# The first tile's x in another order: first weight chunk converted early, two k shifts on GpSimd, and the next k two slots later

## The chip, the cores and the metric

The kernel runs on one core of one Trainium2 chip. The metric is the device time of one execution in microseconds (us); shorter is better. TensorE is called PE here, VectorE DVE, ScalarE ACT, GpSimd POOL and SyncE SP, as in the profile. All four compute engines and SP's DMA queue run their own instruction lists in order and meet at semaphores.

## The reference

A linear attention over q, k and v of 8 batches, 8 heads, 576 positions and 64 columns feeds a two-layer feed-forward over 4608 tokens:

```python
q_s = softmax of q over its 64 columns          # exp(q - max) / (sum + 1e-9)
k_s = softmax of k over its 576 positions
kv  = einsum('bhsd,bhse->bhde', k_s, v)
x   = einsum('bhsd,bhde->bhse', q_s, kv)        # as [4608, 512]
h   = x @ w_in                                  # [4608, 2048]
out = softplus(h) @ w_out                       # [4608, 512]
```

Everything is float32 outside. Weights arrive as float32 bits in 64-bit words and are converted on the chip.

## The kernel before, in words

The 4608 tokens are cut into nine tiles of 512. For each tile the feed-forward runs sixteen **slots**, one for each 128 columns of the hidden layer (a **chunk**). A slot j issues, in this order: the up-projection of chunk j on PE (`up`, L367 in the first tile, L372 to L374 later), the attention steps of the next tile that a table puts into this slot, the conversion steps of the coming weight chunks, softplus of chunk j (`softplus`, L384 to L390 on ACT and DVE), and the down-projection of chunk j - 2 (`down`, L412). Products on PE that an attention step needs are gathered (`later`) and issued at the end of the slot. The work of one slot on each engine stands in that engine's list in the order of this code; no scheduler moves it.

**The weights.** In the first tile each chunk must be converted before it is used. `top_w` (L120) and `scale_w` (L115) on ACT, `sign_w` on DVE (L126) or, for chunks 0 and 1, on POOL (L128), and last `join_w` on DVE (L136). `top_w` reads both halves of a chunk, so it waits for the load of w_in and of w_out. Chunks 0 and 1 are converted ahead of the slots, chunk j + 2 after softplus of slot j, and `join_w(j + 1)` stands between the attention steps and softplus of slot j. Up-projection j + 1 waits for it.

**The attention.** `kv_unit` makes kv for one batch and two heads (index h, four per batch). Its steps are numbered u*h*0 to u*h*5: `top` (maximum over chunks of k, L182, and a transpose on PE, L184), `across` (maximum over the partitions, L198, and a transpose back, L199), `shift` (k minus its maximum, L203), `product` (exp on ACT, L209, twenty matmuls, L214), `scale` (L224, L225) and `keep` (L232) or `split` (L238, L241). `q_unit` has twelve steps q0 to q11: maxima (L278), an exchange between partition blocks (`swapped`, four small copies into the tile `other`, L265) with L287, the shift (L290), exp (L293), sums (L296), the second exchange and the reciprocal (L300, L301), and the division (L304). `x_first` makes x of the first tile, steps x*h*0 to x*h*2: `flip` (transpose, L348), `product` (L351), `take` (copy to x0, L355 on ACT, L357 on DVE).

**The head of the program**, up to the first up-projection, is a string of step names written out by hand; each name appends its instructions to the lists of the engines. t, m, s and j with a digit are `top_w`, `scale_w`, `sign_w` on POOL and `join_w` of chunk 0 or 1, "kv", "w" and "q" issue loads. k of the first batch lies in the tiles kvt, kvt, x_130 and x_136 for h = 0 to 3. In `attend(1)` the four kv units of the second batch are spread over the slots of the first tile from slot 2h on, two slots apart; each one's product also starts a later k load into the buffer that it frees.

Of the kernel before, what the change touches and what calls it, by code (L numbers as in the profile page):

```python
# [8 lines left out]
F32 = mybir.dt.float32  # L9
# [10 lines left out]
P = 128  # L20
B, H, S, D = 8, 8, 576, 64
DM, DF = 512, 2048
NT = B * S
HP = H // 2
# [30 lines left out]
def tile_attn_ffn(  # L55
# [9 lines left out]
    nc = tc.nc  # L65
# [8 lines left out]
    sm = ctx.enter_context(tc.tile_pool(name="sm", bufs=1))  # L74
# [76 lines left out]
    def later(products):  # L151
        if waiting is None:
            products()
        else:
            waiting.append(products)
# [14 lines left out]
        queue.dma_start(out=t[0:TAIL, NCH, :, 0:2 * D], in_=kv_tail[b, h])  # L170
        return t

    def kv_unit(b, h, bank, after=None):

        t = loaded.pop((b, h))
        kt, vt = t[:, :, :, 0:D], t[:, :, :, D:KVW]
        wide, ps = bank[:, 0:P], bank[:, 0:D + 1]
        state = {}

        def top():  # L180
            mx = sm.tile([P, 2, D], F32, name="mx", bufs=2)
            nc.vector.tensor_reduce(out=mx, in_=kt.rearrange("p c z d -> p z d c"), op=ALU.max, axis=AX.X)  # L182
            if b <= ON_PE:
                later(lambda: nc.tensor.transpose(wide, mx.rearrange("p z d -> p (z d)"), ident))  # L184
                return
            mb = sm.tile([P, 2, D], F32, name="mx", bufs=2)
            nc.gpsimd.partition_all_reduce(
                mb.rearrange("p z d -> p (z d)"), mx.rearrange("p z d -> p (z d)"), channels=P,
                reduce_op=bass_isa.ReduceOp.max,
            )  # L190
            state["mb"] = mb

        def across():

            if b > ON_PE:
                return
            m1 = sm.tile([P, 1], F32, name="m1", bufs=2)
            nc.vector.tensor_reduce(out=m1, in_=wide, op=ALU.max, axis=AX.X)  # L198
            later(lambda: nc.tensor.transpose(wide, m1.broadcast_to([P, P]), ident))  # L199

        def shift():
            mb = wide.rearrange("p (z d) -> p z d", z=2) if b <= ON_PE else state["mb"]
            nc.vector.tensor_tensor(  # L203
                out=kt, in0=kt, in1=mb.unsqueeze(1).broadcast_to([P, NCH + 1, 2, D]), op=ALU.subtract
            )

        def product():
            cz = t.rearrange("p c z w -> p (c z) w")[:, :, 0:D]
            nc.scalar.activation(cz, cz, AF.Exp)  # L209

            def products():
                for c in range(NCH + 1):
                    for z in range(2):
                        nc.tensor.matmul(  # L214
                            ps[z * D:(z + 1) * D], lhsT=kt[:, c, z], rhs=vt[:, c, z], start=c == 0, stop=c == NCH
                        )
                if after:
                    after()

            later(products)  # L220

        def scale():
            r = sm.tile([P, 1], F32, name="r", bufs=2)
            nc.vector.tensor_scalar(out=r, in0=ps[:, D:D + 1], scalar1=EPS, scalar2=W_SCALE, op0=ALU.add, op1=ALU.mult)  # L224
            nc.vector.reciprocal(r, r)  # L225
            state["r"] = r

        def keep():

            for z in range(2):  # L230
                zs = slice(z * D, (z + 1) * D)
                nc.scalar.activation(whole[zs, h, zs], ps[zs, 0:D], AF.Copy, scale=state["r"][zs])  # L232

        def split():
            hi, lo, r = kv_hi[b % 2][h], kv_lo[b % 2][h], state["r"]
            for z in range(2):
                zs = slice(z * D, (z + 1) * D)
                nc.scalar.activation(hi[zs, zs], ps[zs, 0:D], AF.Copy, scale=r[zs])  # L238
            for z in range(2):
                zs = slice(z * D, (z + 1) * D)  # L240
                nc.vector.scalar_tensor_tensor(  # L241
                    out=lo[zs, zs], in0=ps[zs, 0:D], scalar=r[zs], in1=hi[zs, zs].bitcast(F32),
                    op0=ALU.mult, op1=ALU.subtract,
                )

        return [top, across, shift, product, scale, split if b else keep]

    def split_whole(h):
# [11 lines left out]
    def swapped(m, copy=nc.vector.tensor_copy):  # L260

        o = sm.tile([P, TOK // 8], F32, name="other")
        for a in range(4):
            z = a ^ 1
            copy(o[32 * a:32 * a + 32], m[32 * z:32 * z + 32])  # L265
        return o

    def q_unit(t):

        n = TOK // 16  # L270
        half = [qtiles[t][:, 2 * g:2 * g + 2].rearrange("p h (i r) -> p (h i) r", r=32) for g in range(2)]
        m, s = (sm.tile([P, TOK // 8], F32, name=name) for name in ("m", "s"))

        def spread(a, g):
            return a[:, g * n:(g + 1) * n].unsqueeze(2).broadcast_to([P, n, 32])

        def top(g):
            nc.vector.tensor_reduce(out=m[:, g * n:(g + 1) * n], in_=half[g], op=ALU.max, axis=AX.X)  # L278

        copy = nc.vector.tensor_copy if t else nc.scalar.copy  # L280
        if t:
            slow = [nc.gpsimd if t == 1 else nc.vector] * 2
        else:
            slow = [nc.vector, nc.gpsimd]

        def join():
            nc.vector.tensor_tensor(out=m, in0=m, in1=swapped(m, copy), op=ALU.max)  # L287

        def shift(g):
            slow[g].tensor_tensor(out=half[g], in0=half[g], in1=spread(m, g), op=ALU.subtract)  # L290

        def power(g):
            nc.scalar.activation(half[g], half[g], AF.Exp)  # L293

        def total(g):
            nc.vector.tensor_reduce(out=s[:, g * n:(g + 1) * n], in_=half[g], op=ALU.add, axis=AX.X)  # L296

        def invert():
            o = swapped(s, copy)
            nc.vector.scalar_tensor_tensor(out=s, in0=s, scalar=EPS, in1=o, op0=ALU.add, op1=ALU.add)  # L300
            nc.vector.reciprocal(s, s)  # L301

        def divide(g):
            slow[g].tensor_tensor(out=half[g], in0=half[g], in1=spread(s, g), op=ALU.mult)  # L304

        return [
            lambda: top(0), lambda: top(1), join, lambda: shift(0), lambda: shift(1),
            lambda: power(0), lambda: power(1), lambda: total(0), lambda: total(1), invert, lambda: divide(0), lambda: divide(1),
        ]
# [131 lines left out]
    with tc.manual_schedule():  # L441
# [17 lines left out]


        po = [ps_o.tile([P, DM], F32, name=f"po{h}") for h in range(HP)]
        units = [kv_unit(0, h, po[h]) for h in range(HP)]
        first = [x_first(h, po[h]) for h in range(HP)]
        todo = {f"q{i}": fn for i, fn in enumerate(q_unit(0))}
        for h in range(HP):
            todo.update({f"u{h}{i}": fn for i, fn in enumerate(units[h])})
# [5 lines left out]
        todo["w"] = lambda: [load_w(k) for k in range(5, 10)]  # L472
        todo["q"] = lambda: [q_load(1)] + [load_w(k) for k in range(10, NJ)]
        for name in (
            "q0 q1 u00 q2 q3 q4 q5 u10 u01 u11 u02 u12 q6 u03 u13 u20 u30 u21 u31 u22 u32 u23 u33 t0 m0 s0 q7 q8 "
            "kv kv w u04 u14 u05 u15 q9 q10 q11 x00 x10 x01 x11 u24 u34 u25 u35 x20 x30 x02 x12 t1 m1 s1 x21 x31 j0 "
            "x22 x32 q"
        ).split():
            todo[name]()

        def attend(t):

            steps = [[] for _ in range(NJ + 1)]

            def lazy(make, slots):
                unit = []

                def step(i):
                    def fn():
                        if not i:  # L490
                            unit.extend(make())
                        unit[i]()
                    return fn

                for i, s in enumerate(slots):
                    steps[s].append(step(i))

            if t < B:
                on_pe = 1 if t <= ON_PE else 0
                for h in range(HP):  # L500
                    a = 2 * h
                    lazy(
                        lambda h=h: kv_unit(t, h, banks[h % 2], after=kv_prefetch),
                        [a, a + on_pe, a + 1 + on_pe, a + 2 + on_pe, a + 3 + on_pe, a + 3 + on_pe],
                    )
            lazy(lambda: q_unit(t), [3, 4, 5, 5, 6, 7, 8, 7, 8, 9, 9, 10])
            for h, slots in enumerate(([11, 11, 12], [12, 12, 13], [13, 13, NJ], [14, 14, NJ])):
                lazy(lambda h=h: x_unit(t, h, banks[h % 2]), slots)
            if t + 1 < NTILE:
                steps[14].append(lambda: q_load(t + 1))  # L510
            return steps
# [3 lines left out]
        for n in range(len(order) + 3):  # L515
            slot = order[n] if n < len(order) else None
            if slot:
                t, j = slot
# [66 lines left out]
```

## Time and profile before

| | |
|---|---|
| time, median of 3 runs | 929.53 us (928.31 to 929.96) |
| the profiled execution's own time | 928.47 us |
| its span | 926.6 us |
| PE busy | 886.7 us, 96% of the span |
| DVE / ACT / POOL busy | 703.8 (76%) / 581.7 (63%) / 56.4 (6%) us |
| first up-projection starts | 34.55 us |
| first up-projection of the second tile starts | about 160.6 us |

The span is the time from the first to the last instruction; the execution's own time is 1.87 us longer. PE is busy nearly throughout from the second tile on, so the time is PE's work plus what PE waits for in the head and in the first tile. PEclk on the page is the clock granted to TensorE in tenths; it stood at half (0.50, which is 1.2 instead of 2.4 GHz) from about 26 to 32 us and again from about 46 to 49 us.

### The profile page before, as it was taken

Reading aid. Unit: us, or ns where it says so; the run is one execution under the profiler, and the core shown is the slowest. Engines: PE = TensorE matmul, PEld = TensorE weight load, DVE = VectorE, ACT = ScalarE, POOL = GpSimd, SP = SyncE. Lnnn points to the kernel's source line nnn. Section 1 sums busy time; section 2 is a strip of 40 time slices with the busy share of each in tenths; the row PEclk is TensorE's granted clock in tenths of the full one; section 3 lists DMA queues with packets and bytes.
Section 4 is the critical chain, followed back from the end, with each engine's and each line's share of the span. In section 5 each row is a group of like instructions: output and inputs, shape, how many; then the busy total and the mean of one; then the engine's idle time right before and its main releaser. Section 6 shows DMA issues by size and latency. Waiting matters only on the chain.

```text
span 926.6 us, 11575 instructions
## 1 busy us (share of the span) xinstructions
PE 886.7 (96%) x4180; PEld 675.3 (73%) x4180; DVE 703.8 (76%) x1095; ACT 581.7 (63%) x982; POOL 56.4 (6%) x118
## 2 busy tenths in 40 slices
PE   2698999999899999999999999999999999999998
PEld 2243444677688888888888888888888888888886
DVE  8679888788878877787778778877787757765553
ACT  3666676756666656666567566656665666566554
POOL 1302200000001100110011000100110000000000
PEclk9899999999999999999999999999999999999999
DMA  9970101111013101210121012101200110001001
GB/s 315 381 298 26 35 17 46 45 53 52 1 46 97 52 1 46 89 43 18 46 71 52 27 46 71 52 26 46 71 27 1 46 46 1 1 1 46 0 1 46
DMA packets 49034, 55.28 MB, mean 60 GB/s; under 512 B 2256, under 2 KB 39120, under 8 KB 47824
## 3 DMA queue, kind: packets, MB, share of 16 engines
q1 hardware_dynamic: 48400, 54.27, 17.4%
q8 instruction: 33, 0.54, 0.2%
q10 hardware_dynamic: 576, 0.26, 0.1%
q14 instruction: 25, 0.20, 0.1%
HBM read 45.09 MB, written 9.44 MB: 59 GB/s over the span
## 4 chain that ended last, share of the span: by engine, by line
PE 76%; DVE 12%; ACT 8%; issue 3%; DMA 1%; POOL 0%; SPq 0%; DVEq 0%; ACTq 0%; POOLq 0%
PE ph L372 11%; PE ph L374 11%; PE ph L373 11%; PE po L418 11%; PE po L416 11%; PE po L417 11%; PE ph L367 3%; PE po L412 3%; PE att L214 2%; DVE w L126 1%; DVE l L390 1%; DVE w L389 1%; DVE w L388 1%; PE att L331 1%; ACT u L385 1%
## 5 line engine op out<-in xcount | busy, mean ns | idle before, releaser
L372 PE MATMUL ph<-x,w 128*128 128x512 f32 x480 | 191.7, 399 | 0.0
L418 PE MATMUL po<-w,g_lo 128*128 128x512 f32 x480 | 187.0, 390 | 1.4 <-DVE g_lo L396 1.4
L374 PE MATMUL ph<-x,w 128*128 128x512 f32 x480 | 188.0, 392 | 0.0
L373 PE MATMUL ph<-x,w 128*128 128x512 f32 x480 | 187.6, 391 | 0.0
L416 PE MATMUL po<-w,g_hi 128*128 128x512 f32 x480 | 186.8, 389 | 0.0
L417 PE MATMUL po<-w,g_hi 128*128 128x512 f32 x480 | 186.7, 389 | 0.0
L388 DVE SCALAR_TENSOR_TENSOR w<-w,u 128x512 f32<-128x512 f32 x128 | 88.4, 691 | 108.8 <-ACT w L386 108.8
L395 ACT CAST g_hi<-l 128x512 fp32r<-128x512 f32 x128 | 79.7, 622 | 92.3 <-DVE l L390 89.8
L390 DVE SCALAR_TENSOR_TENSOR l<-l,ln,w 128x512 f32<-128x512 f32 x128 | 96.3, 752 | 15.7 <-DVE w L389 1.4
L418 PEld LDWEIGHTS po<-w,g_lo 128*128 128x128 f32 x480 | 90.1, 188 | 21.2 <-DVE g_lo L396 2.6
L372 PEld LDWEIGHTS ph<-x,w 128*128 128x128 f32 x480 | 90.8, 189 | 19.3 <-issue 0.6
L374 PEld LDWEIGHTS ph<-x,w 128*128 128x128 f32 x480 | 90.4, 188 | 19.7
L417 PEld LDWEIGHTS po<-w,g_hi 128*128 128x128 f32 x480 | 90.1, 188 | 18.7
L416 PEld LDWEIGHTS po<-w,g_hi 128*128 128x128 f32 x480 | 90.1, 188 | 18.6
L373 PEld LDWEIGHTS ph<-x,w 128*128 128x128 f32 x480 | 90.7, 189 | 17.6 <-DVE w L146 0.2
L384 ACT ACTIVATE u<-ph 128x512 f32<-128x512 f32 x134 | 80.1, 598 | 33.5 <-PE ph L374 25.0
L396 DVE TENSOR_TENSOR g_lo<-l,g_hi 128x512 fp32r<-128x512 f32 x128 | 88.4, 691 | 15.5 <-ACT g_hi L395 15.3
L387 ACT ACTIVATE l<-u 128x512 f32<-128x512 f32 x128 | 79.3, 619 | 25.8 <-DVE g_lo L396 25.2
L389 DVE SCALAR_TENSOR_TENSOR w<-ph,w 128x512 f32<-128x512 f32 x128 | 88.5, 691 | 4.4
L385 ACT ACTIVATE u<-u 128x512 f32<-128x512 f32 x134 | 84.7, 632 | 4.3
L386 ACT ACTIVATE w<-u 128x512 f32<-128x512 f32 x128 | 80.9, 632 | 4.1
L325 ACT CAST q_hi<-att 128x512 fp32r<-128x512 f32 x32 | 18.8, 587 | 78.6 <-DVE att L321 78.6
(125 smaller groups left out, 1061.1 us busy)
## 6 DMA issues: line engine op xcount, KB each, us to landing
kvt<-in_kv SPq DMA_DIRECT2D x30, 512.0 KB, 4.2
qt<-in_q SPq DMA_DIRECT2D x9, 1024.0 KB, 4.9
w<-in_w_in SPq DMA_DIRECT2D x16, 512.0 KB, 10.2
w<-in_w_out SPq DMA_DIRECT2D x16, 512.0 KB, 10.2
out<-w SPq DMA_DIRECT2D x32, 256.0 KB, 2.3
kvt<-in_kv_tail SPq DMA_DIRECT2D x28, 64.0 KB, 3.9
x<-in_kv SPq DMA_DIRECT2D x2, 512.0 KB, 9.4
out<-x SPq DMA_DIRECT2D x4, 256.0 KB, 2.4
```

The source lines that it names most:

```text
L372: nc.tensor.matmul(ph, lhsT=w_hi, rhs=x_hi, start=h == 0, stop=False)
L373: nc.tensor.matmul(ph, lhsT=w_lo, rhs=x_hi, start=False, stop=False)
L374: nc.tensor.matmul(ph, lhsT=w_hi, rhs=x_lo, start=False, stop=h == HP - 1)
L385: nc.scalar.activation(u, u, AF.Exp, scale=-1.0)
L386: nc.scalar.activation(w, u, AF.Copy, bias=1.0)
L388: nc.vector.scalar_tensor_tensor(out=w, in0=w, scalar=1.0, in1=u, op0=ALU.subtract, op1=ALU.subtract)
L389: nc.vector.scalar_tensor_tensor(out=w, in0=ph, scalar=0.0, in1=w, op0=ALU.max, op1=ALU.subtract)
L390: nc.vector.scalar_tensor_tensor(out=l, in0=l, scalar=ln1, in1=w, op0=ALU.subtract, op1=ALU.add)
L396: nc.vector.tensor_tensor(out=g_lo, in0=l, in1=g_hi.bitcast(F32), op=ALU.subtract)
L416: nc.tensor.matmul(po, lhsT=g_hi[:, ms], rhs=w_hi, start=j == 0, stop=False)
L417: nc.tensor.matmul(po, lhsT=g_hi[:, ms], rhs=w_lo, start=False, stop=False)
L418: nc.tensor.matmul(po, lhsT=g_lo[:, ms], rhs=w_hi, start=False, stop=j == NJ - 1)
```

## The change

Four edits. (1) The string of steps in the head is written in another order: t0 and m0 (the conversion of chunk 0 on ACT) stand right behind the exp of the first half of q, s0 (POOL) before the exp of the second half; the sums' exchange (q9) stands between the work of h = 0 and h = 1; j0 before the last flips; t1, m1, s1 behind the last flips. (2) The shifts of h = 2 and 3 are done by POOL instead of DVE; ACT first copies their maxima from PSUM into the tile mx, which POOL reads. (3) For the second tile's q the exchange copies are on ACT. (4) In the first tile the kv units of the second batch start two slots later.

```diff
--- before.py
+++ after.py
@@ -170,7 +170,7 @@
         queue.dma_start(out=t[0:TAIL, NCH, :, 0:2 * D], in_=kv_tail[b, h])
         return t
 
-    def kv_unit(b, h, bank, after=None):
+    def kv_unit(b, h, bank, engine=nc.vector, after=None):
 
         t = loaded.pop((b, h))
         kt, vt = t[:, :, :, 0:D], t[:, :, :, D:KVW]
@@ -200,7 +200,10 @@
 
         def shift():
             mb = wide.rearrange("p (z d) -> p z d", z=2) if b <= ON_PE else state["mb"]
-            nc.vector.tensor_tensor(
+            if engine is nc.gpsimd:
+                mb = sm.tile([P, 2, D], F32, name="mx", bufs=2)
+                nc.scalar.copy(mb.rearrange("p z d -> p (z d)"), wide)
+            engine.tensor_tensor(
                 out=kt, in0=kt, in1=mb.unsqueeze(1).broadcast_to([P, NCH + 1, 2, D]), op=ALU.subtract
             )
 
@@ -277,7 +280,7 @@
         def top(g):
             nc.vector.tensor_reduce(out=m[:, g * n:(g + 1) * n], in_=half[g], op=ALU.max, axis=AX.X)
 
-        copy = nc.vector.tensor_copy if t else nc.scalar.copy
+        copy = nc.vector.tensor_copy if t > 1 else nc.scalar.copy
         if t:
             slow = [nc.gpsimd if t == 1 else nc.vector] * 2
         else:
@@ -459,7 +462,7 @@
 
 
         po = [ps_o.tile([P, DM], F32, name=f"po{h}") for h in range(HP)]
-        units = [kv_unit(0, h, po[h]) for h in range(HP)]
+        units = [kv_unit(0, h, po[h], engine=nc.vector if h < 2 else nc.gpsimd) for h in range(HP)]
         first = [x_first(h, po[h]) for h in range(HP)]
         todo = {f"q{i}": fn for i, fn in enumerate(q_unit(0))}
         for h in range(HP):
@@ -472,9 +475,8 @@
         todo["w"] = lambda: [load_w(k) for k in range(5, 10)]
         todo["q"] = lambda: [q_load(1)] + [load_w(k) for k in range(10, NJ)]
         for name in (
-            "q0 q1 u00 q2 q3 q4 q5 u10 u01 u11 u02 u12 q6 u03 u13 u20 u30 u21 u31 u22 u32 u23 u33 t0 m0 s0 q7 q8 "
-            "kv kv w u04 u14 u05 u15 q9 q10 q11 x00 x10 x01 x11 u24 u34 u25 u35 x20 x30 x02 x12 t1 m1 s1 x21 x31 j0 "
-            "x22 x32 q"
+            "q0 q1 u00 q2 q3 q4 q5 t0 m0 u10 u01 u11 u02 u12 s0 q6 u03 u13 u20 u30 u21 u31 u22 u32 q7 q8 kv kv w u23 "
+            "u04 u05 q9 u33 u14 u15 q10 q11 x00 x10 x01 x11 j0 x02 u24 u25 u34 u35 x20 x30 x21 x31 x12 t1 m1 s1 x22 x32 q"
         ).split():
             todo[name]()
 
@@ -498,7 +500,7 @@
             if t < B:
                 on_pe = 1 if t <= ON_PE else 0
                 for h in range(HP):
-                    a = 2 * h
+                    a = 2 * h + (2 if t == 1 else 0)
                     lazy(
                         lambda h=h: kv_unit(t, h, banks[h % 2], after=kv_prefetch),
                         [a, a + on_pe, a + 1 + on_pe, a + 2 + on_pe, a + 3 + on_pe, a + 3 + on_pe],
```

On ACT, in the head, before: from the first copies of q's exchange (other<-m) to the second exchange (other<-s). The tile w_142 is chunk 0, spare holds kv, po_179 to po_182 are the PSUM banks of h = 0 to 3.

```order
L265 COPY other<-m 32x64 x4
L293 ACTIVATE qt<-qt 128x1024 x2
L209 ACTIVATE kvt<-kvt 128x10x64 x2
L209 ACTIVATE x_130<-x_130 128x10x64
L209 ACTIVATE x_136<-x_136 128x10x64
L120 ACTIVATE w_142<-w_142 128x1024
L115 ACTIVATE w_142<-w_142 128x1024
L232 ACTIVATE spare<-po_179,r 64x64 x2
L232 ACTIVATE spare<-po_180,r 64x64 x2
L265 COPY other<-s 32x64 x4
```

The same stretch of ACT's list with the change:

```order
L268 COPY other<-m 32x64 x4
L296 ACTIVATE qt<-qt 128x1024
L120 ACTIVATE w_142<-w_142 128x1024
L115 ACTIVATE w_142<-w_142 128x1024
L296 ACTIVATE qt<-qt 128x1024
L212 ACTIVATE kvt<-kvt 128x10x64 x2
L205 COPY mx<-po_181 128x128
L205 COPY mx<-po_182 128x128
L212 ACTIVATE x_130<-x_130 128x10x64
L235 ACTIVATE spare<-po_179,r 64x64 x2
L268 COPY other<-s 32x64 x4
L212 ACTIVATE x_136<-x_136 128x10x64
```

The two instructions on w_142 moved from behind the exps of all four k tiles to a place ahead of the second exp of qt and of all four; two copies into mx are new; the keeping of po_180 went behind the second exchange.

On DVE, in the head, before: from the sums of q to the first flips (w_160 holds the flipped q).

```order
L296 TENSOR_REDUCE s<-qt 128x32 x2
L224 TENSOR_SCALAR r<-po_179 128x1
L225 RECIPROCAL r<-r 128x1
L224 TENSOR_SCALAR r<-po_180 128x1
L225 RECIPROCAL r<-r 128x1
L300 SCALAR_TENSOR_TENSOR s<-s,other 128x64
L301 RECIPROCAL s<-s 128x64
L304 TENSOR_TENSOR qt<-qt,s 128x1024
L348 STREAM_TRANSPOSE w_160<-qt 128x512 x2
```

The same with the change:

```order
L299 TENSOR_REDUCE s<-qt 128x32 x2
L227 TENSOR_SCALAR r<-po_179 128x1
L228 RECIPROCAL r<-r 128x1
L303 SCALAR_TENSOR_TENSOR s<-s,other 128x64
L304 RECIPROCAL s<-s 128x64
L227 TENSOR_SCALAR r<-po_180 128x1
L228 RECIPROCAL r<-r 128x1
L307 TENSOR_TENSOR qt<-qt,s 128x1024
L351 STREAM_TRANSPOSE w_160<-qt 128x512 x2
L136 SCALAR_TENSOR_TENSOR w_142<-w_142 128x1024
```

The two shifts of x_130 and x_136 that stood ahead of these rows are gone from DVE; the sums' reciprocal now stands before the scaling of po_180, and the join of chunk 0 stands behind the first two flips.

On DVE, in slot 8 of the first tile, before: from the end of softplus to the join of the next chunk. att_105 and att_106 are the two PSUM banks of the kv units.

```order
L390 SCALAR_TENSOR_TENSOR g_hi<-g_hi,ln_109,g_lo 128x512
L126 TENSOR_SCALAR w_298<-w_298 128x1024
L224 TENSOR_SCALAR r<-att_105 128x1
L225 RECIPROCAL r<-r 128x1
L241 SCALAR_TENSOR_TENSOR kv_lo_103<-att_105,r,kv_hi_95 64x64 x2
L203 TENSOR_TENSOR kvt<-kvt,att_106 128x10x64
L296 TENSOR_REDUCE s<-qt 128x32
L136 SCALAR_TENSOR_TENSOR w_298<-w_298 128x1024
```

The same with the change:

```order
L393 SCALAR_TENSOR_TENSOR g_hi<-g_hi,ln_109,g_lo 128x512
L126 TENSOR_SCALAR w_280<-w_280 128x1024
L227 TENSOR_SCALAR r<-att_106 128x1
L228 RECIPROCAL r<-r 128x1
L244 SCALAR_TENSOR_TENSOR kv_lo_102<-att_106,r,kv_hi_94 64x64 x2
L206 TENSOR_TENSOR kvt<-kvt,att_105 128x10x64
L182 TENSOR_REDUCE mx<-kvt 128x128
L299 TENSOR_REDUCE s<-qt 128x32
L136 SCALAR_TENSOR_TENSOR w_280<-w_280 128x1024
```

The units' numbers moved on by one (what was h = 2 is h = 1), and a maximum over k, of h = 3, stands between the shift and the sums; before, that one stood two slots earlier.

## Rows read from the trace of the kernel before

**Rows 1.** The windows view, in stages; columns: stretch, length, each engine's busy time, clock, DMA

```profile
0.00:34.55 34.55, 12.42 (x96) 7.21 (x97) 26.64 (x66) 15.96 (x30) 9.21 (x16) 0.90 1.03 327
34.55:160.63 126.08, 117.96 (x352) 52.45 (x353) 105.80 (x141) 84.34 (x122) 13.20 (x17) 0.99 0.31 116
160.63:926.60 765.97, 756.34 (x3734) 615.67 (x3732) 571.33 (x890) 481.43 (x830) 33.94 (x86) 1.00 0.12 38
```

**Rows 2.** One load by its tile: the issue of w_out's first block, and its landing

```profile
L97 SPq DMA_DIRECT2D w<-in_w_out x1: 432/432/432, 10.9 to 10.9; - x1
...
DMA to landing us min/median/max: 6.3/6.3/6.3
```

**Rows 3.** The timeline of ACT, 13 to 26 us; columns: start, duration, instruction, [wait before it]

```profile
13.60 1.06 ACT L293 ACTIVATE qt<-qt 128x1024 f32<-128x1024 f32 x1 [1.12 <-POOL qt L290]
14.56 1.36 ACT L209 ACTIVATE kvt<-kvt 128x640 f32<-128x640 f32 x2
19.94 1.48 ACT L209 ACTIVATE x<-x 128x640 f32<-128x640 f32 x2 [4.02 <-DVE x L203]
21.33 1.14 ACT L120 ACTIVATE w<-w 128x1024 uint32<-128x1024 uint8 x1
22.36 1.12 ACT L115 ACTIVATE w<-w 128x1024 f32<-128x1024 f32 x1
...
24.68 1.00 ACT L265 COPY other<-s 32x64 f32<-32x64 f32 x4
```

**Rows 4.** The timeline of PE, 15 to 39 us

```profile
15.34 2.44 PE L214 MATMUL po<-kvt 128*64 128x65 f32 x40 [1.37 <-ACT kvt L209]
...
18.57 0.59 PE L199 MATMUL po<-ident,m 128*128 128x128 f32 x2 [0.17 <-DVE m L198]
20.74 1.54 PE L214 MATMUL po<-x 128*64 128x65 f32 x40 [1.58 <-ACT x L209]
28.68 5.60 PE L351 MATMUL po<-w,spare 128*128 128x512 f32 x8 [6.40 <-DVE w L348]
34.55 3.68 PE L367 MATMUL ph<-x,w 128*128 128x512 f32 x8 [0.27 <-DVE w L136]
```

**Rows 5.** The timeline of DVE, 20 to 30 us

```profile
20.55 2.34 DVE L296 TENSOR_REDUCE s<-qt 128x32 f32<-128x1024 f32 x2
...
26.57 1.23 DVE L304 TENSOR_TENSOR qt<-qt,s 128x1024 f32<-128x1024 f32 x1
27.82 1.30 DVE L348 STREAM_TRANSPOSE w<-qt 128x512 f32<-128x512 f32 x2
```

**Rows 6.** The timeline of POOL, three of its operations

```profile
11.66 1.90 POOL L290 TENSOR_TENSOR qt<-qt,m 128x1024 f32<-128x1024 f32 x1
...
23.58 2.46 POOL L128 TENSOR_SCALAR w<-w 128x1024 bf16<-128x1024 f32 x1 [10.02 <-ACT w L115]
...
80.64 1.92 POOL L290 TENSOR_TENSOR qt<-qt,m 128x1024 f32<-128x1024 f32 x1
```

**Rows 7.** The timeline of DVE in the first tile's slots

```profile
77.63 2.24 DVE L388 SCALAR_TENSOR_TENSOR g_lo<-g_lo,l 128x512 f32<-128x512 f32 x1
...
80.71 2.40 DVE L390 SCALAR_TENSOR_TENSOR g_hi<-g_hi,ln,g_lo 128x512 f32<-128x512 f32 x1
...
86.66 1.29 DVE L182 TENSOR_REDUCE mx<-kvt 128x128 f32<-128x640 f32 x1
...
100.33 0.20 DVE L224 TENSOR_SCALAR r<-att 128x1 f32<-128x1 f32 x1
...
102.12 0.82 DVE L203 TENSOR_TENSOR kvt<-kvt,att 128x640 f32<-128x640 f32 x1
```

**Rows 8.** The timeline of PE in the first tile: three up-projections that waited

```profile
45.55 5.41 PE L367 MATMUL ph<-x,w 128*128 128x512 f32 x8 [1.01 <-DVE w L136]
...
71.93 3.71 PE L367 MATMUL ph<-x,w 128*128 128x512 f32 x8 [2.09 <-DVE w L136]
...
105.26 3.71 PE L367 MATMUL ph<-x,w 128*128 128x512 f32 x8 [0.79 <-DVE w L136]
```

## The prediction, made before the changed kernel was run

> **What bounds the kernel now.** I read the page's busy shares first, then the windows by stage, and then each engine's timeline of the first 160 us. From 160.63 us on PE is busy 756.34 of 765.97 us, and the change leaves the instructions of that stage and their order as they are [rows 1]. What it can move lies before: 34.55 us of head, in which PE works 12.42, and 126.08 us of the first tile, in which it works 117.96 [rows 1]. In the head the reader is to see a string of hand-overs: exps of k on ACT, products and transposes on PE, maxima and shifts on DVE, the conversion of chunk 0, the second exchange on ACT, the division and the flips on DVE, and then four products at 28.68 that run slowly, 5.60 us for eight instructions of 512 columns where the same shape takes 3.68 right after [rows 3 to 5]. The 6.40 us of idle PE ahead of them, and the page's clock, say that this is the lower level, 1.2 GHz. In the first tile, up-projections wait for the join of their chunk on DVE, the third, sixth and tenth for instance [rows 8]; how long depends on the attention steps that stand ahead of that join.
>
> **The head, step by step.** The part that decides is the conversion of chunk 0 on ACT. Before, it stands at 21.33 and takes 2.04 us to the next instruction's start, on the chain [rows 3]. Now it stands ahead of the second exp of q and the exps of h = 0 and 1. It reads the whole chunk, and its second half was issued at 10.9 and landed 6.3 later, at 17.2 [rows 2]. SP's list is the same, so that load lands then again. ACT has nothing it may do between the first exp of q, over at 12.48 (13.60 less its wait of 1.12) [rows 3], and 17.2. All exps behind wait: L120 at 17.2, L115 at 18.25, second exp of q at 19.25, exps of h = 0 and 1 at 20.2 to 21.6, where they ran from 14.56 to 15.92 [rows 3]. That is 5.7 late.
>
> PE's list has the transposes of h = 2 and 3 behind the products of h = 0 and 1, so they are late by the same: products 21.0 to 23.4, last transposes from 24.2 to 24.8 instead of 18.57 to 19.16 [rows 4]. DVE's two small maxima wait for them, and q's sums stand behind these: sums from 24.4 to 26.7 instead of 20.55 to 22.89 [rows 5], 3.8 late (two DVE shifts less, worth 1.5 and their wait).
>
> ACT then copies the two maxima (128x128 out of PSUM). The trace has no such copy; it lies between the 0.25 of a small copy (1.00 for four) and the 0.74 of a 640-column exp [rows 3]; I take 0.3. POOL shifts x_130. POOL's shift of 1024 columns of q took 1.90 alone [rows 6], 1.19 by columns; the upper end is the 2.46 of its other whole operation [rows 6]. I take 1.2, since the operation is the same: 25.1 to 26.4. ACT's list goes on with that tile's exp (0.74), the keeping of h = 0 (0.62), and the four exchange copies (1.00): these start at 27.7, where they started at 24.68 [rows 3]. From the copies' start to the division DVE took 1.89 before (24.68 to 26.57) [rows 3, 5]; now 0.3 of scaling of h = 1 comes between: 29.9.
>
> There it meets POOL. POOL's own half of the division starts as soon as the reciprocal is there, at 29.6, and now before DVE's. The trace shows what such a meeting costs: L390, usually 0.75, started at 80.71 beside a POOL operation of 80.64 to 82.56 and took 2.40, that is to 0.55 after POOL's end [rows 6, 7]; L388 at 77.63 did likewise. So DVE's half ends near 32.6 instead of 31.1. Both ends of this price, 0 and 1.5, stay in the range; I take 1.5, since both meetings on record were paid in full.
>
> The Trainium skill, SBUF — State Buffer, section Who interferes with whom, says that a VectorE instruction with two SBUF inputs and a GpSimd one that reads SBUF take a shared port by turns, the first for its whole instruction. By that rule the sum is as here, and without it 1.5 less; the rows on L390 agree. The skill's GPSIMD Engine Reference, section 3.1, gives 4497 ns for a GpSimd tensor_tensor of 2048 columns; worked out for 640 that is an estimate of 1.4, and by it the sum would be 0.2 more.
>
> The first two flips take 0.65 each (1.30 for two) [rows 5]; the first product on PE follows the first flip at 33.5, and PE is again fresh from idling. With 5.87 from there to the first up-projection as before (28.68 to 34.55) [rows 4] that starts at 39.2 to 39.4, less what overlaps: 39.15. The join of chunk 0, 1.2, is now hidden behind those products. Conversion of chunk 1 ends on ACT near 38.9, POOL's sign (2.46) [rows 6] and the join follow until 42.6, just as the first up-projection ends. **Head: 39.15 - 34.55 = +4.6.**
>
> **The first tile, step by step.** Slot by slot against before:
> - Slots 1 and 3, third and fifth up-projection: DVE has one small reduction less ahead of the join (0.2), with 0.1 of transposes: -0.3. The third still waits over 3.5 us of idle PE, so its 5.41 (upper level: 3.68) [rows 4, 8] stays.
> - Slot 4: the scaling and splitting of h = 0 leave, 1.79 from L224 at 100.33 to the shift at 102.12 in the like slot [rows 7]. PE loses a product there too (half of 1.54, 0.77) [rows 4], so the wait of 2.09 [rows 8] shrinks by 1.0 and the product's own time turns up again in slot 11: -1.0.
> - Slot 6: a k load's fills now come later on POOL, since they wait for that product; so POOL's second shift no longer starts just ahead of L390. That saves between 0 and 1.65 (2.40 - 0.75) [rows 7]; I take two thirds, as ACT's conversion is next to be late: -1.1.
> - Slot 8: one maximum over k more, 1.29 [rows 7], ahead of a join that PE waited 0.79 for already [rows 8]: +1.2.
> - Slot 10: one shift more, 0.82 [rows 7], in a slot with no slack: +0.75.
> - Slot 12: scaling and splitting of h = 3 come in, 1.79, partly beside the product of slot 11 (0.77): +1.1.
> - Exchange copies on ACT take 0.8 off DVE in slots 5 and 9, where PE did not wait: 0.
> **Tile: -0.3 - 1.0 - 1.1 + 1.2 + 0.75 + 1.1 = +0.65.** Each of these could be off by its own size; -2 to +3 for all.
>
> **Sum.** +4.6 + 0.65 = +5.25. The profiled execution took 928.47 (926.6 of span and 1.87 around it) and would take 933.7. It lies 1.06 under the median of 929.53, at the low end of the three runs; on the median the sum gives 934.8, which I forecast.
>
> **The rivals.**
> - *The meetings go well.* DVE's division does not wait for POOL (-1.5), or the scattered products of k between 21 and 30 us keep PE at the upper level, where the four products take 3.7 instead of 5.6; of these 1.9 about 1.1 reaches the slots, since the join of chunk 1 is next to be late. For it: the second pair of k products ran at 1.54 where the first took 2.44 [rows 4], so PE speeds up within the head. Against: PE idles some 3 us ahead of the products in any case. About -3 together at most: +2.3, 931.8.
> - *The late slots cost more.* Slots 8 to 12 hold the division, flips and splits besides, and POOL's shifts may take the 2.46 of the upper end (+1.3 in the chain): +8.5, 938.
> - *ACT's wait reaches nothing.* ACT idled 4.02 us before the exps of x_130 and x_136 anyway [rows 3], and 2.04 of conversion leave the chain. If the second k pair does not hang on the first one's exps, the head gets 2.0 shorter, with the join (1.2) hidden too: -3.2 and +0.65 for the tile, 927.0. It decides where the transposes of h = 2 and 3 could pass the products of h = 0 and 1; PE's list has them behind, which speaks against it.
> - *The slots decide.* Moving the k units by two slots does away with the waits of the sixth and tenth up-projections (2.09 + 0.79) and the slow third (1.73) without giving anything back in slots 8 to 12, and no meeting with POOL (head +3.1): -1.5, 928.0. The moved steps must fit late slots; slot 8's wait of 0.79 [rows 8] says that they don't.
>
> **How the numbers follow.** Forecast 0.62 (its own range 932.8 to 937), meetings go well 0.16, late slots cost more 0.10, ACT's wait reaches nothing 0.06, the slots decide 0.06. The measurement tells about 0.2%, 1.9 us, from no change. Slower by more: 0.62 + 0.10 and two thirds of 0.16, 0.83. Within: the rest of 0.16 and most of the last, 0.10. Faster: 0.07. The range of 930.6 to 938 leaves out the two faster cases and the tail above.
>
> **What would show it.** ACT's L120 on chunk 0 with a wait of 4 to 5 us that ends by a load, near 17.2; exps of kvt near 20.2; DVE idle some 6 us from 17.3 until the maxima of h = 2 and 3; DVE's half of the division with over 2 us; first up-projection between 38 and 40; waits of PE in slots 8, 10 and 12 longer than before and in slot 4 shorter. The prediction is wrong if the first up-projection starts before 37, or if the first tile's length differs from 126.08 by more than 3.

## The result, and the profile after

The changed kernel takes 933.39 us, the median of 7 runs (931.76 to 937.32); the kernel before took 929.89 us in 7 runs (928.31 to 929.98) taken beside it. The ratio is 1.0048, with a 95% interval of 1.0031 to 1.0065: slower by some 3.5 us. The forecast was 934.8. The profiled execution of the changed kernel is its shortest, 931.76 us with a span of 930.0, 3.4 longer than the span before. The lines below are of that execution; from L203 on, numbers of lines are 3 higher than before (L367 is now L370). One execution timed for e5 below ran at a granted clock of 0.565 and took 1493.49 us; the ratio there leaves it out.

The windows by stage (length, busy time and count of PE, PEld, DVE, ACT and POOL, granted clock, DMA share, GB/s; PEld is PE's loading of weights) are cut at the first up-projection and at the start of the second tile, as [rows 1] are:

```profile
0.00:38.92 38.92, 13.34 (x96) 7.81 (x97) 26.34 (x63) 15.45 (x31) 10.78 (x17) 0.87 1.03 338
38.92:163.97 125.05, 115.95 (x353) 51.86 (x352) 101.03 (x133) 87.43 (x132) 13.79 (x17) 1.00 0.28 102
163.97:930.00 766.03, 755.24 (x3734) 614.55 (x3732) 571.18 (x890) 481.85 (x830) 34.10 (x86) 1.00 0.12 38
```

The head grew by 4.37 us (38.92 against 34.55), the first tile shrank by 1.03 (125.05 against 126.08), and the rest is as long as before within 0.1. So in this execution the whole loss sits in the head. ACT's timeline there (start, duration, engine, line, operation, shapes, count, and in brackets the idle time before and what ended it), against [rows 3]:

```profile
17.01 1.14 ACT L120 ACTIVATE w<-w 128x1024 uint32<-128x1024 uint8 x1 [4.86 <-DMA w<-in_w_out]
...
19.99 1.36 ACT L212 ACTIVATE kvt<-kvt 128x640 f32<-128x640 f32 x2
24.36 0.48 ACT L205 COPY mx<-po 128x128 f32<-128x128 f32 x2 [3.00 <-PE po L199]
26.19 0.75 ACT L212 ACTIVATE x<-x 128x640 f32<-128x640 f32 x1 [1.35 <-POOL x L206]
```

ACT stands idle for 4.86 us at L120 until the second half of weight chunk 0 lands, and the exps of kvt start at 19.99 instead of 14.56. The delay runs on through PE, DVE and POOL. PE's timeline, against [rows 4, 8]:

```profile
20.77 2.44 PE L217 MATMUL po<-kvt 128*64 128x65 f32 x40 [7.09 <-ACT kvt L212]
...
33.18 5.90 PE L354 MATMUL po<-w,spare 128*128 128x512 f32 x8 [2.54 <-DVE w L351]
38.92 3.60 PE L370 MATMUL ph<-x,w 128*128 128x512 f32 x8
43.24 3.71 PE L370 MATMUL ph<-x,w 128*128 128x512 f32 x8 [0.72 <-DVE w L136]
49.73 3.71 PE L370 MATMUL ph<-x,w 128*128 128x512 f32 x8 [2.79 <-DVE w L136]
...
72.64 3.71 PE L370 MATMUL ph<-x,w 128*128 128x512 f32 x8 [1.19 <-DVE w L136]
...
106.58 3.71 PE L370 MATMUL ph<-x,w 128*128 128x512 f32 x8 [1.90 <-DVE w L136]
```

DVE's timeline, against [rows 5, 7]:

```profile
23.65 0.51 DVE L198 TENSOR_REDUCE m<-po 128x1 f32<-128x128 f32 x2 [6.67 <-PE po L184]
24.07 2.34 DVE L299 TENSOR_REDUCE s<-qt 128x32 f32<-128x1024 f32 x2
...
29.45 2.93 DVE L307 TENSOR_TENSOR qt<-qt,s 128x1024 f32<-128x1024 f32 x1
...
80.64 0.75 DVE L393 SCALAR_TENSOR_TENSOR g_hi<-g_hi,ln,g_lo 128x512 f32<-128x512 f32 x1 [0.28 <-ACT g_hi L390]
82.73 1.72 DVE L126 TENSOR_SCALAR w<-w 128x1024 uint8<-128x1024 uint8 x1 [1.33 <-ACT w L115]
```

And POOL's, against [rows 6]:

```profile
24.70 2.86 POOL L206 TENSOR_TENSOR x<-x,mx 128x640 f32<-128x640 f32 x2 [2.99 <-ACT mx L205]
...
29.39 1.91 POOL L307 TENSOR_TENSOR qt<-qt,s 128x1024 f32<-128x1024 f32 x1 [0.66 <-DVE r L227]
```

DVE waits 6.67 us for the transposes that PE's list holds behind the late products. Its division starts 0.06 behind POOL's and takes 2.93. In slot 6, L393 takes its usual 0.75, where the same instruction met POOL before [rows 7].

### The profile page after: what moved, and what is told of

It is laid out like the page before. It is cut to its first block, busy times and chain, and to the rows that moved or that the text cites. A ratio compares the mean times of both kernels' runs of the same rounds, so it can differ in the third digit from the quotient of the medians.

```text
span 930.0 us, 11575 instructions
## 1 busy us (share of the span) xinstructions
PE 884.5 (95%) x4180; PEld 674.2 (72%) x4180; DVE 698.5 (75%) x1085; ACT 584.7 (63%) x992; POOL 58.7 (6%) x120
## 4 chain that ended last, share of the span: by engine, by line
PE 76%; DVE 11%; ACT 7%; DMA 2%; issue 2%; POOL 0%; SPq 0%; DVEq 0%; ACTq 0%; POOLq 0%
PE ph L375 11%; PE ph L377 11%; PE ph L376 11%; PE po L421 11%; PE po L419 11%; PE po L420 11%; PE po L415 3%; PE ph L370 3%; PE att L217 2%; DVE l L393 1%; DVE w L392 1%; DMA w<-in_w_out 1%; DVE w L126 1%; DVE w L391 1%; PE att L334 1%
## 5 line engine op out<-in xcount | busy, mean ns | idle before, releaser
L393 DVE SCALAR_TENSOR_TENSOR l<-l,ln,w 128x512 f32<-128x512 f32 x128 | 96.3, 752 | 15.3 <-DVE w L392 0.9
```

Of the source, the lines that this page charges most:

```text
L393: nc.vector.scalar_tensor_tensor(out=l, in0=l, scalar=ln1, in1=w, op0=ALU.subtract, op1=ALU.add)
```

## The experiments

The theory: **ACT's early conversion** stops its list until the load lands, and this alone is the loss. The rivals: the shifts on POOL and the division's meeting with it set the head; or the later slots cost the time. "Before" on the three chips used was 929.22 (e1 to e4), 929.06 (e5 to e8) and 929.21 us (e9 to e11).

### e1: the conversion of chunk 0 back behind the exps

```diff
-"... q5 t0 m0 u10 u01 u11 u02 u12 s0 q6 u03 u13 u20 u30 u21 u31 u22 u32 q7 ..."
+"... q5 u10 u01 u11 u02 u12 q6 u03 u13 t0 m0 u20 u30 u21 u31 u22 u32 s0 q7 ..."
```

> The changed kernel, but chunk 0's conversion stands on ACT behind the exps of h = 0 and 1 (and POOL's sign behind its two shifts). If ACT's wait for the load sets the head: no wait of ACT of 4.86 us, exps of kvt near 14.3 again, exps of x_130 near 21, first up-projection 5 to 6.5 us earlier than the changed kernel's 38.92 (33 to 34), time 926.5 to 929.5. If the shifts on POOL and their copies set it: first up-projection stays within 2 us of 38.92, time 931 or more. If the later slots set the loss: the head is shorter but the time stays above that of the kernel before by 1 to 2 us.

Measured: 928.84 us (926.20 to 931.17, 12 runs), ratio 0.9990 (0.9978 to 1.0002). ACT's timeline in e1:

```profile
14.70 1.36 ACT L212 ACTIVATE kvt<-kvt 128x640 f32<-128x640 f32 x2
17.26 1.14 ACT L120 ACTIVATE w<-w 128x1024 uint32<-128x1024 uint8 x1 [1.20 <-DMA w<-in_w_out]
```

PE's timeline in e1:

```profile
33.20 3.60 PE L370 MATMUL ph<-x,w 128*128 128x512 f32 x8
...
102.56 5.40 PE L370 MATMUL ph<-x,w 128*128 128x512 f32 x8 [1.89 <-DVE w L136]
```

The conversion still begins when the load lands, but the exps no longer stand behind it. The first up-projection starts 5.7 us earlier than in the changed kernel, and the loss is gone: 6.0 us less than the changed kernel on the same chip (934.81, e4). All other edits of the change together are within measurement of no change; e5 takes them apart further.

### e2: the kernel before, with that conversion early and nothing else

```diff
-"... q5 u10 u01 u11 u02 u12 q6 ... u23 u33 t0 m0 s0 q7 ..."
+"... q5 t0 m0 u10 u01 u11 u02 u12 s0 q6 ... u23 u33 q7 ..."
```

> The kernel before with one edit: chunk 0's conversion right behind the first exp of q. If ACT's wait for the load sets the head: exps of kvt 5.5 us later, q's sums near 26.2, the second exchange near 30 instead of 24.68, first up-projection 4.5 to 5.5 us later than 34.55, time 933.5 to 936. If ACT's idle time hides the conversion: first up-projection 0 to 2 us earlier, time 927.5 to 930.

Measured: 934.74 us (933.58 to 935.03, 4 runs), ratio 1.0056 (1.0041 to 1.0072). ACT's timeline in e2:

```profile
17.15 1.13 ACT L120 ACTIVATE w<-w 128x1024 uint32<-128x1024 uint8 x1 [4.71 <-DMA w<-in_w_out]
```

PE's timeline in e2:

```profile
34.12 5.11 PE L351 MATMUL po<-w,spare 128*128 128x512 f32 x8 [5.39 <-DVE w L348]
39.63 3.68 PE L367 MATMUL ph<-x,w 128*128 128x512 f32 x8 [0.40 <-ACT x L355]
```

One moved conversion makes the same wait, the same head (39.63) and as much loss, 5.5 us, as the whole change. Taken away (e1) and put in alone (e2), it gives the same answer, so the cause is shown. The rival that POOL's shifts set the head falls: here DVE does them, and in e1, where POOL does, the head is 33.20.

### e3: only the k units two slots later

```diff
-a = 2 * h
+a = 2 * h + (2 if t == 1 else 0)
```

> The kernel before with one edit: the k units of the second batch two slots later in the first tile. By the prediction's slots: first up-projection unchanged at 34.55, the first tile (34.55 to 160.63) longer by 0.65 with the third up-projection slow (5.4 us), shorter by about 1 with it at the upper clock; time -1 to +1.5 against before. If the later slots carry the loss of the changed kernel: +3 or more.

Measured: 929.41 us (929.09 to 932.26, 12 runs), ratio 1.0008 (1.0000 to 1.0017). PE's timeline, to be held against [rows 8]:

```profile
45.32 5.41 PE L367 MATMUL ph<-x,w 128*128 128x512 f32 x8 [3.74 <-DVE w L136]
...
69.92 3.71 PE L367 MATMUL ph<-x,w 128*128 128x512 f32 x8 [1.19 <-DVE w L136]
...
104.50 3.71 PE L367 MATMUL ph<-x,w 128*128 128x512 f32 x8 [1.92 <-DVE w L136]
```

The wait of slot 4 falls from 2.09 to 1.19, and that of slot 8 grows from 0.79 to 1.92. The tile is 1.34 longer in this profile (127.42), against a forecast of 0.65; the median rises by 0.2, and the interval begins at no change. The slots don't decide.

### e4: the changed kernel once more, beside e1 to e3

> The changed kernel once more, to see whether its times keep their spread (931.76 to 937.32 in seven runs). If the spread comes from TensorE's clock in the two stretches after an idle PE (the four products of x, the third up-projection): times between 931.5 and 937.5 again, and this profile, unless it is again of the shortest kind, shows the third up-projection at 5.4 instead of 3.7 us. If the spread was chance of one session: within 2 us.

Measured: 934.81 us (934.61 to 936.97, 6 runs), ratio 1.0067 (1.0054 to 1.0080). The profiled execution took 936.97 with a span of 935.2, 5.2 over that of the first profile of the same code. PE's timeline in e4:

```profile
33.49 6.45 PE L354 MATMUL po<-w,spare 128*128 128x512 f32 x8 [2.54 <-DVE w L351]
...
50.58 6.44 PE L370 MATMUL ph<-x,w 128*128 128x512 f32 x8 [3.35 <-DVE w L136]
...
110.21 5.40 PE L370 MATMUL ph<-x,w 128*128 128x512 f32 x8 [1.91 <-DVE w L136]
```

Up to the first product of x it is within 0.3 us of the first profile; what differs behind is how fast PE runs after a wait. The head's end is 0.86 later, the third up-projection 2.73 longer, the tenth 1.69: 5.3 us together, against 5.2 between the spans. Between these two executions, one of the shortest and one of the longest, PE's speed makes nearly the whole difference; the other runs that spread over 5 us have no trace.

### e5 and e6: what is left of the head

e5 is e1 with the slots as before (`a = 2 * h`). e6 is e5 with DVE doing the sign of chunk 0 and the division before the last keeping:

```diff
-"... u22 u32 s0 q7 q8 kv kv w u23 u04 u05 q9 u33 u14 u15 q10 q11 x00 x10 ..."
+"... u22 u32 q7 q8 kv kv w u23 u04 s0 u05 q9 q10 q11 u33 x00 u14 u15 x10 ..."
-lambda k: sign_w(k, nc.gpsimd)
+lambda k: sign_w(k, nc.gpsimd if k else nc.vector)
```

> The kernel of e1 (conversion in ACT's gap) with the k units of the second batch back in their old slots. If the later slots cost only through the longer waits of PE that lower its clock (the tenth up-projection, 5.40 us in two traces): no wait over 1 us in slot 8, tenth up-projection 3.7 us, median 0.5 to 2 us under e1's 928.84, that is 927 to 928.3, and fewer times near 931. If the later slots gain: 929 to 930.

> The kernel of e5, with the sign of chunk 0 on DVE in its wait for the exchange (so that POOL doesn't hold up L303, 1.45 instead of 0.23 us in e1) and DVE's half of the division right behind the reciprocal, ahead of POOL's. If DVE and POOL take turns by who starts first: L303 at 0.23, the division at 1.2 ending near 25.4 (26.8 in e1), POOL's half over 2.5 us, first up-projection 1 to 1.5 us earlier than e5's, time 925.5 to 927.5. If what delays L303 and L307 is another cause (ACT's copies, the reads themselves): no change against e5.

Measured: e5 926.40 us, the median of all nine executions; eight lie from 925.87 to 928.27, with 926.26 in the middle, and give the ratio of 0.9975 (0.9965 to 0.9986). e6: 927.10 us (926.76 to 928.45, 11 runs), ratio 0.9983 (0.9975 to 0.9992). So e5 keeps the good half of the change: without the early conversion and the later slots it beats the kernel before, by more than was forecast. Its tenth up-projection took 3.71 behind 0.79 of waiting, where e1's took 5.40 behind 1.89. The later slots thus seem to have hidden part of that gain in e1, but the intervals of the two ratios overlap, and e3 found little, so this is likely and not shown.

e6's time lies in the range named for it, yet against e5 it gained nothing. The turns came out as expected (DVE's half 1.22, POOL's 2.65), and the first product of x starts at 26.28 against 27.60. With PE also faster in those products (5.50 against 6.42), the first up-projection starts at 31.62 against 33.86, and nothing is left of the 2.2 us. PE's timeline in e5:

```profile
33.86 3.60 PE L370 MATMUL ph<-x,w 128*128 128x512 f32 x8
...
44.79 3.71 PE L370 MATMUL ph<-x,w 128*128 128x512 f32 x8 [1.00 <-DVE w L136]
```

PE's timeline in e6 shows where they went:

```profile
31.62 3.60 PE L370 MATMUL ph<-x,w 128*128 128x512 f32 x8
...
36.38 3.71 PE L370 MATMUL ph<-x,w 128*128 128x512 f32 x8 [1.06 <-DVE w L136]
...
42.55 5.41 PE L370 MATMUL ph<-x,w 128*128 128x512 f32 x8 [1.01 <-DVE w L136]
```

DVE's timeline in e6, in slot 4:

```profile
65.65 1.28 DVE L182 TENSOR_REDUCE mx<-kvt 128x128 f32<-128x640 f32 x1 [0.46 <-DMA kvt<-in_kv_tail]
```

The second up-projection now waits 1.06 for its join. The third ran slowly where e5's took 3.71, which gave back 1.7. And in slot 4 DVE waits for a load of k that lands no sooner: its maximum starts at 65.65 here and at 65.94 in e5. An earlier start only runs into it. The second tile starts only 0.33 earlier (159.24 against 159.57).

### e7 and e9: hold the clock, then bring the load forward

e7 is e6 with extra 128-column matmuls of the identity, whose results nobody reads: 8 and 4 and 4 in the gaps of the head, 12 behind the second up-projection. e9 is e7 with the loads of weight chunks 12 to 15 issued behind the next k load instead of ahead of it (the product of h = 0 of the second batch starts them):

```diff
+def fill(n, bank):
+    for _ in range(n):
+        nc.tensor.matmul(bank[:, 0:P], lhsT=ident, rhs=ident, start=True, stop=True)
...
-[q_load(1)] + [load_w(k) for k in range(10, NJ)]
+[q_load(1)] + [load_w(k) for k in range(10, 12)]
+def first_prefetch():
+    kv_prefetch()
+    for k in range(12, NJ):
+        load_w(k)
```

> The kernel of e6 with extra matmuls on the identity, whose results nobody reads, in three places of the head where PE idles (8, 4 and 4) and behind the second up-projection (12). If the slow products of x and the slow third up-projection come from PE's idle time ahead of them: the eight instructions of the products at 3.5 to 4.5 instead of 5.7 us, the third up-projection at 3.7 in the profile, times in one group, 923 to 925.5. If the clock there depends on something else: 5.4 us stay, and the time is e6's or up to 1 us more for the extra matmuls.

> The kernel of e7, with the loads of weight chunks 12 to 15 issued behind the k load that the second batch's first product starts, not ahead of it. If that k load in a full DMA queue took back what e7 gained (maximum over k of h = 2 waited 2.44 us for the tail's load, sixth up-projection at 69.81): no such wait, sixth up-projection 1.5 to 2.5 us earlier, near 67.7, its clock at the upper level, time 924 to 926.5 against e7's 928.15. If the extra matmuls themselves cost the time: 927.5 to 928.5 again.

Measured: e7 928.15 us (927.62 to 928.81, 11 runs), ratio 0.9991 (0.9982 to 1.0000). e9: 923.24 us (922.96 to 925.07, 5 runs), ratio 0.9939 (0.9925 to 0.9953). DVE's timeline in e7:

```profile
66.00 1.30 DVE L182 TENSOR_REDUCE mx<-kvt 128x128 f32<-128x640 f32 x1 [2.44 <-DMA kvt<-in_kv_tail]
```

PE's timeline in e7:

```profile
29.82 1.95 PE L354 MATMUL po<-w,spare 128*128 128x512 f32 x4 [1.31 <-DVE w L351]
...
42.59 3.71 PE L370 MATMUL ph<-x,w 128*128 128x512 f32 x8
...
69.81 5.98 PE L370 MATMUL ph<-x,w 128*128 128x512 f32 x8 [2.12 <-DVE w L136]
```

DVE's timeline in e9:

```profile
63.19 1.29 DVE L182 TENSOR_REDUCE mx<-kvt 128x128 f32<-128x640 f32 x1
```

PE's timeline in e9:

```profile
67.00 3.71 PE L370 MATMUL ph<-x,w 128*128 128x512 f32 x8 [2.08 <-DVE w L136]
```

e7 is a miss. The extra matmuls do what they are for: four instructions of the products of x take 1.95, and the third up-projection 3.71. The head is no shorter for it in this profile: the second pair of products waits 1.31 for DVE's flips, and the first up-projection starts at 31.62 as in e6. And DVE then reaches the load of k sooner, and waits 2.44 us for it; PE slows behind that wait, and e7 is no faster than e6. The windows from 42 to 60 us (columns as above) show what the load stands behind. In e7:

```profile
42.00:60.00 18.00, 18.00 (x66) 8.41 (x65) 15.06 (x21) 12.60 (x18) 0.47 (x3) 1.00 1.03 411
```

In e9:

```profile
42.00:60.00 18.00, 18.00 (x65) 8.36 (x64) 15.10 (x21) 12.37 (x18) 0.46 (x3) 1.00 0.59 231
```

The DMA engines are full in e7 until the weights are in. With four chunks moved behind k, the wait is gone, the sixth up-projection starts 2.8 earlier and takes 3.71 instead of 5.98 (granted clock from 60 to 80 us: 1.00 in e9, 0.83 in e7), and the time falls by 4.9, more than forecast. The extra matmuls pay nothing while that load is late.

### e8: the changed kernel with DVE's half of the division first

```diff
-"u04 u05 q9 u33 u14 u15 q10 q11 x00 ..."
+"u04 u05 q9 q10 q11 u33 u14 u15 x00 ..."
```

> The changed kernel with one edit: DVE's half of the division directly behind the reciprocal, ahead of the scaling of h = 1. If the meeting with POOL cost 1.5 us: L307 at 1.2 instead of 2.93 us, POOL's half at about 3 instead of 1.91, first up-projection 1 to 1.8 us before 38.92 (39.78 in the second trace), time 932 to 934. If it was hidden: within 0.5 us of the changed kernel's start.

Measured: 930.86 us (930.50 to 933.35, 9 runs), ratio 1.0029 (1.0019 to 1.0038): below the 932 to 934 expected. DVE's timeline in e8:

```profile
29.70 1.22 DVE L307 TENSOR_TENSOR qt<-qt,s 128x1024 f32<-128x1024 f32 x1
```

POOL's timeline in e8:

```profile
29.75 2.95 POOL L307 TENSOR_TENSOR qt<-qt,s 128x1024 f32<-128x1024 f32 x1 [0.67 <-DMA kvt<-in_kv_tail]
```

PE's timeline in e8:

```profile
31.86 6.38 PE L354 MATMUL po<-w,spare 128*128 128x512 f32 x8 [0.86 <-DVE w L351]
38.08 3.60 PE L370 MATMUL ph<-x,w 128*128 128x512 f32 x8
```

Only the order differs, and now DVE's half takes 1.22 and POOL's 2.95, where it was 2.93 and 1.91. (The bracket of POOL's line names a load, but the division needs DVE's reciprocal, which was over at 29.66.) The half that starts first runs through, the second ends late. The Trainium skill (SBUF — State Buffer, Who interferes with whom) says that the order of issue decides who blocks; both traces agree. The first product of x is ready 1.32 earlier than in the changed kernel's first profile (31.86 against 33.18), though POOL's shifts start 0.36 later; the products then run 0.5 slower (6.38 against 5.90), and the head is 0.84 shorter. The spans of these two profiles, both with a third up-projection of 3.71, differ by 1.0 (929.0 and 930.0); e8's median lies further below the changed kernel's two, 2.5 and 4.0, and how much of that is PE's speed in the other runs is open.

### e10 and e11: chunk 1 converted early

e10 is e6 (no extra matmuls) and e11 is e9, each with `t1 m1 s1` right behind `u33`; e10 has e9's order of loads too.

> The kernel of e6 (no extra matmuls) with the k load ahead of chunks 12 to 15 as in e9, and the conversion of chunk 1 right behind the exp of x_136 instead of behind the flips. By the chain as understood: second up-projection directly behind the first (it waited 1.06 us), no wait for the k load's tail (0.46), 1 to 1.5 us less than e6's 927.1 where the clock stays as there, 925 to 926.5. If the clock after the waits decides alone: two groups of times some 1.7 us apart, and the median within 0.5 us of e6's.

> All of it: e9 and the early conversion of chunk 1. By the chain as understood 1 us less than e9, 923 to 925.5, below both kernels by 0.4% or more. If DVE's flips (they hold the third product of x in e7, 1.31 us) and the third up-projection's conversion bound the start anyway: as e9.

Measured: e10 926.75 us (924.58 to 927.58, 6 runs), ratio 0.9968 (0.9956 to 0.9980). e11: 923.19 us (923.07 to 923.63, 5 runs), ratio 0.9934 (0.9922 to 0.9947). PE's timeline in e10:

```profile
33.27 3.60 PE L370 MATMUL ph<-x,w 128*128 128x512 f32 x8
...
44.19 6.53 PE L370 MATMUL ph<-x,w 128*128 128x512 f32 x8 [1.01 <-DVE w L136]
```

PE's timeline in e11:

```profile
31.46 3.60 PE L370 MATMUL ph<-x,w 128*128 128x512 f32 x8
...
35.00 3.61 PE L370 MATMUL ph<-x,w 128*128 128x512 f32 x8
...
42.41 3.71 PE L370 MATMUL ph<-x,w 128*128 128x512 f32 x8 [1.01 <-DVE w L136]
```

The second up-projection no longer waits (35.00 against e9's 35.97), but the third starts where it did (42.41 against 42.32): its own join is now last, and e11 equals e9. What sets e10 and e11 apart is the extra matmuls: in the two profiles 1.8 us in the head (e10's products of x took 6.74) and 2.8 in the third up-projection, which is all of the 4.5 between their spans (925.8 and 921.3). e10's profile is of its longest execution and e11's of its shortest; the medians lie 3.6 apart. e10 is a miss: neither the load of k nor the second join holds it any more, and its median is still within 0.4 of e6's, as the rival had it, though its times do not fall into two groups. Neither the extra matmuls alone (e7) nor the load's order with chunk 1 early (e10) brought more than 0.4 against e6; matmuls and order together (e9) brought 3.9. e9 and e11 are the best versions seen, 6.0 us below the kernel before.

## Why the prediction was right, step by step

**ACT's wait** was forecast at 4 to 5 us from a load landing at 17.2; it was 4.86, until 17.01. The exps of kvt were to come at 20.2 and came at 19.99; q's sums at 24.4, and came at 24.07, behind a DVE idle time of 6.67. e1 and e2 show that this step is the cause.

**POOL's shifts** were put at 1.2 each and took 1.43 (2.86 for two). By the 4497 ns that the Trainium skill (GPSIMD Engine Reference, 3.1) gives for 2048 columns the estimate was 1.4, and this trace agrees with it. ACT's copy was put at 0.3 and took 0.24. Both errors are hidden by the start being 0.4 earlier (24.70 against 25.1): the exp came at 26.19, where 26.4 was forecast.

**The meeting with POOL** was charged in full, and came in full: from 29.45 to 32.38, with 32.6 forecast. The first product followed at 33.18 (33.5), slow again, 5.90 (5.60 before), and the first up-projection at 38.92 (39.15). Head: +4.37 against +4.6.

**The slots** came to +0.67 without the clock, against +0.65, and by parts less well. From the starts of the up-projections in both traces (the length of a slot after, less that before): the product of h = 0, 0.80 long, left slot 3 (the forecast had slot 4) and came back in slot 11. With it, slots 0 and 1 together gave -0.19, slot 3 -0.87 and slot 11 +0.75: -0.31 in all (forecast -0.3). Slot 4 gave -0.91 (-1.0), slot 6 -0.61 (-1.1), slot 8 +1.22 (+1.2), slots 9 and 10 +0.41 (+0.75), slot 12 and behind +0.86 (+1.1). The meeting on L393 in slot 6 did vanish, but DVE then waits 1.33 for ACT's L115, and its L126 takes 1.72 instead of 1.31, so the gain reached PE only in part. The sum is right by cancellation of terms that are off by up to 0.5.

**The step that failed** is the one on the third up-projection, that its 5.41 "stays". In this execution it took 3.71 behind a wait of 2.79, so the tile came out at -1.03 instead of +0.65. In e4 the same instructions took 6.44, and the tile was 129.28 long, +3.20. The forecast treated the clock behind a wait as fixed; it varies between executions of the same code, and the median of 933.39 lies among them. So the forecast's 934.8 is 1.4 above the first median and equal to that of e4. The head was foreseen by its mechanism; that the whole came this near is partly luck, since it hangs on which level an execution draws. How often each is drawn is open.

**The rivals.** "ACT's wait reaches nothing" (927.0) and "the slots decide" (928.0) fell with e1 to e3. "The meetings go well" fell in both halves: the products of x took 5.90, and the meeting was paid. To avoid it takes the other order: in e8, where DVE goes first, the first product comes 1.32 earlier, close to the 1.5 that the forecast put on the meeting. "The late slots cost more" (938) is what the longest runs look like, 937.32 and 936.97, but in the one that has a trace (936.97, e4) it is PE's lower level behind waits and not the work in the slots that makes it so.

## What to carry to other kernels

On an engine that works through its list in order, an instruction may be moved up only as far as its last operand is there: look up when the load lands, and who stands behind the instruction. When several waits of a few us follow each other, taking one away is worth only what the next one leaves, so look for the next (here a join, a load behind 4 MB of weights, PE's lower level) before building. Time a kernel of this kind several times, and read the profile of a long run beside that of a short one.

## What the runs showed of the hardware

The clock behind waits of 1 to 3 us is not the same from one execution to the next. The third up-projection took 3.71 after 2.79 us of waiting (changed kernel) and 6.44 after 3.35 (e4, the same code; granted clock 0.50 from 51.3 to 54.7 us). It took 3.71 after 3.25 (e8) and after 2.10 and 1.00 on either side of one transpose (e5), and 5.41 after 1.12 and 1.01 on either side of it (e6). With the extra matmuls and no load to wait for, five runs of e11 lie within 0.56 us, and its mean granted clock is 0.999.

The granted clock's record can miss the lower level at the start of a program. In e4's windows (columns as above)

```profile
34.00:37.60 3.60, 3.60 (x5) 1.20 (x4) 3.10 (x9) 1.91 (x6) 0.00 (x0) 1.00 1.03 407
...
51.30:54.70 3.40, 3.40 (x5) 1.35 (x4) 3.29 (x4) 1.39 (x3) 0.00 (x0) 0.50 1.03 410
```

it reads 1.00 from 34.0 to 37.6 us, while PE got through five instructions in 3.6 us, as slowly as from 51.3 to 54.7 where it reads 0.50. In the first profile of the same code it reads 0.50 from 34.2 to 37.6, where five instructions took 3.4 us. There the duration of an instruction is to be believed, and not the record.

POOL and DVE meet in other pairs as well. In e6 the sign of chunk 0 on DVE (L126, at 21.34) took 2.27 beside POOL's shifts instead of 1.31 later on, and the small fill that POOL started at 22.49 took 1.25 instead of 0.20, about until L126 was over. The four later kernels with this edit (e7, e9, e10, e11) show the same, 2.11 to 2.60 and 1.25 to 1.26.
